# Two blocks of rows (64 and 60 per partition) made into one block of 124 in an elementwise kernel that streams three tensors

## The chip, the cores and the metric

The kernel runs on one core of a Trainium2 chip. The metric is device time in microseconds (us) of one execution. A core has several engines that run side by side, each with its own queue of instructions: here VectorE (DVE) does the arithmetic, TensorE (PE) one small matrix product, and the queues of SyncE (SP) and ScalarE (ACT) issue the DMAs. A DMA moves data between HBM, the large memory, and SBUF, the on-chip memory of 128 partitions; 16 DMA engines carry all DMAs of the core, whichever queue issued them. Engines wait for one another, and for DMAs, by semaphores.

## The reference

```python
B, S, D = 1024, 16, 512
x, y: [B, S, D] bf16;  gamma: [D] bf16

def reference(x, y, gamma):
    return x + gamma * y
```

The three tensors are taken as 16384 rows of 512 numbers. A row is 1 KiB, a tensor 16.8 MB; x and y are read and the output is written, 50.3 MB in all. gamma is the same for each row, so it doesn't matter which partition works on which row, as long as x, y and the output agree.

## The kernel before

Each of the 128 partitions works on 128 rows of y, which all lie in SBUF at once (`y_sb`, 128 KiB a partition, local rows 0 to 127). The result overwrites y there. x has a smaller tile, `x_sb` of 76 rows a partition, whose places are used twice.

*Which rows of the tensors a partition holds* is set by `BLOCKS` (line 7). The tensor is cut into blocks in HBM: the first 4 x 128 rows, then 64 x 128, then 60 x 128. Within a block, partition p has consecutive rows: 4 of the first, 64 of the second, 60 of the third. `rows_of` (line 65) makes the HBM side of a transfer of the local rows a to b: it looks for the block that holds them, views it as "(p n) d -> p n d", and takes the rows from it. Each partition's part of a transfer is one contiguous run in HBM, and the distance from one partition's run to the next, here called the pitch, is the block's rows times 1 KiB:

```python
c = max(c for c in range(len(BLOCKS)) if edges[c] <= a)
assert b <= edges[c + 1]
block = t[P * edges[c] : P * edges[c + 1]].rearrange("(p n) d -> p n d", p=P)
return block[:, a - edges[c] : b - edges[c], :]
```

*The transfers* are two lists in local rows, each the order of one queue. `x` and `y` are loads, `g` the load of gamma, `s` a store; the fourth number of an x load is its place in `x_sb`:

```python
SP  = [('y', 0, 4), ('y', 4, 68), ('x', 4, 68, 4), ('y', 68, 128), ('x', 68, 120, 24), ('x', 120, 128, 0)]
ACT = [('x', 0, 4, 0), ('g',), ('s', 4, 68), ('s', 0, 4), ('s', 68, 128)]
```

`ring` (line 113) issues them. The first two of SP and the first of ACT are moved ahead of the program's opening barriers (`EARLY`, lines 197 to 203); the next ones wait until the load of y rows 0 to 4 has landed (`HOLD`, line 119). The x loads of rows 68 to 120 and 120 to 128 write places of `x_sb` that earlier rows of x had, so each waits on SP for the additions that read those (`frees`, line 102; wait in line 126). The stores wait until the load of x rows 68 to 120 has landed (`RELEASE`, lines 157 to 159 and 123), and each for the additions of its rows. The semaphore waits are made by `_take` (line 32, with the wait itself in line 35).

*The arithmetic* is five pieces of 8, 16, 44, 52 and 8 local rows (`PIECES`), on VectorE alone: `m` multiplies a piece of y by gamma in place (line 180), `a` adds x to it (line 189), in the order `m0 m1 m2 a2 a0 a1 m3 m4 a3 a4`. Before the first multiplication, TensorE spreads gamma over the 128 partitions by a product with a row of ones (line 152), and VectorE copies it to SBUF (line 154). Each piece waits for the loads that bring its rows.

Of the kernel before, what the change touches and what calls it, by code (L numbers as in the profile page):

```python
# [3 lines left out]

BLOCKS = [4, 64, 60]

PIECES = [8, 16, 44, 52, 8]

# [27 lines left out]
def kernel(  # L38
# [22 lines left out]
    dt = xf.dtype  # L61
    edges = [sum(BLOCKS[:c]) for c in range(len(BLOCKS) + 1)]
    assert edges[-1] == rows

    def rows_of(t, a, b):

        c = max(c for c in range(len(BLOCKS)) if edges[c] <= a)
        assert b <= edges[c + 1]
# [165 lines left out]
```

## Time and profile before

| what | value |
|---|---|
| median of 3 runs | 119.66 us (119.55 to 119.72) |
| the profiled execution's span, first to last instruction | 118.2 us |
| first multiplication starts (y rows 4 to 68 landed) | 23.95 us |
| first addition starts (x rows 4 to 68 landed) | 43.45 us |
| last addition ends | 94.4 us |
| stores issued | 77.4, 77.8 and 94.4 us |
| VectorE busy | 70.1 us |

Times in the profile count from the start of the span. The time of a run is longer than the span by what lies around it. "SPq" and "ACTq" are the queues that issue DMAs; q1 and q10 in the table of DMA queues are SP's and ACT's. A DMA is carried out as packets, and a stretch of the DMA table lists the packets that start in it: how many, how many MB, and the time that they took as a share of what 16 engines have in that stretch. The share can be over 100%, since a packet that starts in a stretch may end after it.

### The profile page before, as it was taken

The numbers are of one execution on the slowest core, as the hardware profiler recorded it, in microseconds if no ns is written. First come the engines' busy times: TensorE is split into PE (matmuls) and PEld (weight loads), VectorE is DVE, ScalarE is ACT, GpSimd is POOL, SyncE is SP. The second block draws the span as 40 slices with busy tenths as digits, with TensorE's granted clock in tenths as the row PEclk, the third lists the DMA queues.
The fourth block names the chain that finished last, engine by engine and source line by source line (L and its number), as shares of the span: only waits on it lengthen the run. The fifth ranks groups of instructions, "written<-read, shape, count | busy, mean of one in ns | idle before, by whom it ended". The sixth has DMA issues, their size and how long they took to land. (4 is left out here: it accounts for less than half of the span.)

```text
span 118.2 us, 91 instructions
## 1 busy us (share of the span) xinstructions
PE 0.6 (0%) x1; PEld 0.1 (0%) x1; DVE 70.1 (59%) x12; POOL 0.2 (0%) x4
## 2 busy tenths in 40 slices
PE   0000100000000000000000000000000000000000
PEld 0000000000000000000000000000000000000000
DVE  0000200089999969999999999999999900000000
POOL 0000000000000000000000000000000000000000
DMA  6999889988899879879969696898899889799793
GB/s 248 461 666 399 355 355 399 665 355 355 355 599 466 355 333 624 374 333 499 499 288 576 288 576 288 360 637 355 355 576 488 355 355 510 333 582 416 333 499 166
DMA packets 1442, 50.33 MB, mean 426 GB/s; under 512 B 161, under 2 KB 162, under 8 KB 546
## 3 DMA queue, kind: packets, MB, share of 16 engines
q1 hardware_dynamic: 864, 33.03, 64.8%
q10 hardware_dynamic: 578, 17.30, 33.9%
HBM read 33.56 MB, written 16.78 MB: 426 GB/s over the span
## 5 line engine op out<-in xcount | busy, mean ns | idle before, releaser
L180 DVE TENSOR_TENSOR y_sb<-y_sb,gamma_sb 128x4096 bf16<-128x4096 bf16 (+3 forms) x5 | 34.7, 6981 | 10.9 <-DVEq L35 10.9
L189 DVE TENSOR_TENSOR y_sb<-x_sb,y_sb 128x4096 bf16<-128x4096 bf16 (+3 forms) x5 | 34.7, 6981 | 1.2 <-DVEq L35 1.1
L154 DVE CAST gamma_sb<-gamma_ps 128x512 bf16<-128x512 f32 x1 | 0.7, 692 | 10.2 <-DVEq L35 10.2
L146 DVE MEMSET ones_row<- 1x128 bf16 x1 | 0.2, 165 | 2.0 <-PEq L51 2.0
L152 PE MATMUL gamma_ps<-gamma_row,ones_row 1*128 1x512 bf16 x1 | 0.6, 581 | 11.6 <-PEq L35 11.6
L152 PEld LDWEIGHTS gamma_ps<-gamma_row,ones_row 1*128 1x128 bf16 x1 | 0.1, 101 | 11.6 <-issue 11.6
L218 POOL MEMSET const-bfloat16-1.0<- 128x1 bf16 x1 | 0.1, 101 | 0.0
L218 POOL MEMSET const-uint8-127<- 128x1 uint8 x1 | 0.1, 101 | 0.0
L218 POOL MEMSET const-float32-0.0<- 128x1 f32 x1 | 0.1, 98 | 0.2 <-issue 0.2
L218 POOL MEMSET const-float32-1.0<- 128x1 f32 x1 | 0.1, 98 | 0.0
## 6 DMA issues: line engine op xcount, KB each, us to landing
y_sb<-in_y_dram SPq DMA_DIRECT2D x1, 7680.0 KB, 57.3
out_dram<-y_sb ACTq DMA_DIRECT2D x1, 7680.0 KB, 23.8
x_sb<-in_x_dram SPq DMA_DIRECT2D x1, 6656.0 KB, 21.7
x_sb<-in_x_dram SPq DMA_DIRECT2D x1, 1024.0 KB, 22.0
y_sb<-in_y_dram SPq DMA_DIRECT2D x1, 512.0 KB, 3.4
x_sb<-in_x_dram ACTq DMA_DIRECT2D x1, 512.0 KB, 4.2
out_dram<-y_sb ACTq DMA_DIRECT2D x1, 512.0 KB, 22.3
y_sb<-in_y_dram SPq DMA_DIRECT2D x1, 23.4
```

The costliest lines, as they stand in the source:

```text
L146: nc.vector.memset(ones_row, 1.0).then_inc(s_ones, 1)
L152: nc.tensor.matmul(gamma_ps, ones_row, gamma_row, start=True, stop=True).then_inc(s_ps, 1)
L154: nc.vector.tensor_copy(out=gamma_sb, in_=gamma_ps).then_inc(s_dve, 1)
L180: nc.vector.tensor_tensor(out=yt, in0=yt, in1=g, op=MULT).then_inc(s_dve, 1)
L189: nc.vector.tensor_tensor(out=yt, in0=xt, in1=yt, op=ADD).then_inc(s_add, 1)
L218: nc = _bacc.Bacc("TRN2", target_bir_lowering=False, num_devices=1)
```

## The change

```diff
-BLOCKS = [4, 64, 60]
+BLOCKS = [4, 124]
```

Nothing else is edited. Behind the first block, partition p now has 124 consecutive rows of the tensors: its local rows 4 to 128. The lists of transfers, in local rows, stay as they are, so a transfer of rows 4 to 68 takes the first 64 of a partition's 124 rows, and one of rows 68 to 128 the last 60. The pitch is 124 KiB for all transfers but those of rows 0 to 4, where it was 64 KiB (rows 4 to 68) or 60 KiB (rows 68 to 128). Before, a transfer of rows 4 to 68 covered one contiguous region of HBM from the first to the last byte; now there are 60 KiB between the runs of neighbouring partitions.

## The prediction

> **What bounds the kernel now.** I read the page's slices first, then its table of queues, then the DMA issues with their time to landing, and last the DMA table again for stretches that hold packets of one transfer alone. From the page:
>
> ```profile
> span 118.2 us, 91 instructions
> PE 0.6 (0%) x1; PEld 0.1 (0%) x1; DVE 70.1 (59%) x12; POOL 0.2 (0%) x4
> DMA  6999889988899879879969696898899889799793
> DMA packets 1442, 50.33 MB, mean 426 GB/s; under 512 B 161, under 2 KB 162, under 8 KB 546
> q1 hardware_dynamic: 864, 33.03, 64.8%
> q10 hardware_dynamic: 578, 17.30, 33.9%
> ```
>
> The two queues' packets fill 64.8 + 33.9 = 98.7% of what 16 DMA engines have in the span. Only the first slice (nothing has arrived) and the last one are much below full. A 7 or a 6 in the middle is not a hole: the profile puts a long packet down in the slice where it starts, and the neighbouring slice shows it (GB/s swings between 288 and 666 likewise). VectorE works 59% of the time. So the kernel lasts as long as the sum of its packets. VectorE would matter only if one of its waits held back an issue until the queues ran dry, and that is read from the issues:
>
> ```profile
> y_sb<-in_y_dram SPq DMA_DIRECT2D x1, 7680.0 KB, 57.3
> out_dram<-y_sb ACTq DMA_DIRECT2D x1, 7680.0 KB, 23.8
> x_sb<-in_x_dram SPq DMA_DIRECT2D x1, 6656.0 KB, 21.7
> out_dram<-y_sb ACTq DMA_DIRECT2D x1, 512.0 KB, 22.3
> 55.37 2.53 SPq L132 DMA_DIRECT2D x_sb<-in_x_dram  x2
> 77.41 17.36 ACTq L138 DMA_DIRECT2D out_dram<-y_sb  x3
> ```
>
> The last two lines are from the timeline (start, duration). The load of x rows 68 to 120 waits for VectorE and is issued at 55.4, while y rows 68 to 128, issued at 4.1, land at 4.1 + 57.3 = 61.4: 6 us of cover. The last store is issued at 77.41 + 17.36 - 0.3 = 94.4, while the store of rows 0 to 4, issued at 77.8, lands at 77.8 + 22.3 = 100.1: 5.7 us of cover. The chain of waits names two additions of VectorE and "issue"; it stops at the last addition, which ends 24 us before the span does, so it doesn't tell what bounds.
>
> The price of one packet, from the DMA table cut to stretches (us), in this order: 3.6 to 23 (y rows 4 to 68), 24 to 42 (x rows 4 to 68), 44 to 60 (y rows 68 to 128), 62 to 74 (x rows 68 to 120), 81 to 98 (store of rows 4 to 68), 101 to 115 (store of rows 68 to 128):
>
> ```profile
> q1 hardware_dynamic: 128, 8.39, 100.4%
> ...
> q1 hardware_dynamic: 112, 7.34, 94.1%
> ...
> q1 hardware_dynamic: 112, 6.88, 99.4%
> ...
> q1 hardware_dynamic: 96, 5.11, 98.3%
> ...
> q10 hardware_dynamic: 112, 7.34, 99.6%
> ...
> q10 hardware_dynamic: 96, 5.90, 97.2%
> ```
>
> Each line has packets, MB and the share of 16 engines. 19.4 us x 16 x 1.004 / 128 = 2.435 us a packet; by the same working 2.420, 2.272, 1.966, 2.419 and 2.268 us. MB over packets gives 65.5, 61.4 and 53.2 KB: one packet is the whole run of one partition (64, 60 or 52 rows of 1 KiB), 128 packets a transfer, 8 on each of 16 engines. In bytes per ns and engine these are 26.9, 27.1, 27.0, 27.1, 27.1 and 27.1. So one rate holds for loads and stores and for a pitch (distance in HBM from one partition's run to the next) of 64 KiB and of 60 KiB.
>
> **The change part by part.** It *removes and adds* no instruction: on every engine the built program has the same instructions in the same order, shapes and waits. No step moves past another on SP, ACT or any queue, and the tile in SBUF keeps its places, since rows 0 to 128 of a partition stay where they were; each partition merely holds other rows of the tensors. What changes is the HBM side of seven transfers: the pitch goes from 64 KiB (three of them) and 60 KiB (four) to 124 KiB, and the start moves for the 60-row part. The run of one partition stays contiguous, 64, 60, 52 or 8 rows. The three transfers of rows 0 to 4 and gamma are untouched.
>
> Seven transfers of 8 packets per engine, priced by the rows above (for the 8-row load 1.966 x 8 / 52 = 0.30): 8 x (2.435 + 2.420 + 2.272 + 1.966 + 0.30 + 2.419 + 2.268) = 8 x 14.08 = 112.6 us of the span's 118.2. That is all the change can touch; the other 5.6 us are the start, the 4-row transfers and the last landing.
>
> *Number of packets: no change, 0 us.* A packet was one partition's run already in the blocks of 64, where neighbouring partitions touch in HBM and longer packets would have been possible; the new layout gives the same runs.
>
> *Price of a packet at a pitch of 124 KiB: not shown by this trace.* Bound below: the cheapest row is 27.1 bytes per ns. The stores show it, and so do most loads; if all reached it, y rows 4 to 68 would give back 8 x (2.435 - 2.419) = 0.13 us, x rows 4 to 68 0.01, y rows 68 to 128 8 x (2.272 - 2.268) = 0.03: some 0.17 in all. Bound above: the dearest. A stretch from 3.6 to 6 us, the first round of packets after the queues fill, has
>
> ```profile
> q1 hardware_dynamic: 16, 1.05, 103.4%
> ```
>
> so 2.4 x 16 x 1.034 / 16 = 2.482 us a packet, 2.6% over 2.419; on all 112.6 us that is +2.9. Between these I take 0. One of the two pitches shown is a power of two (64 KiB) and one is not (60 KiB), as 124 KiB is not; they differ by nothing in stores and by 0.2% or less in the later loads. The one dear transfer is the first big one, dearest in its first round, while x rows 4 to 68 with the same pitch pay 2.420: that goes by when it runs, not by where it lies, so the pitch doesn't remove it.
>
> The row of the first transfer also bears on a rule: the Trainium skill (DMA: Bandwidth & Descriptors, Latency and other measured facts) says that copies whose partitions lie a large power of two apart lose rate, 207 GB/s at 512 KiB against 214 at a padded pitch, and advises padding by a few KiB or laying tiles out contiguously. The change goes against the second half (the blocks of 64 were contiguous as a whole) and with the first (124 KiB is no power of two). With the page's 3% as an estimate for a bad pitch the sum would be +3.5 us or so; the rows at 64 and 60 KiB, equal within 0.2% in steady state, say about 0, and no row has 124 KiB.
>
> *Waits.* Unchanged in number. If packets grow, the waits of VectorE move with them: its first multiplication starts at 23.95 on the landing of y rows 4 to 68 and would start later by 8 times the growth; the covers of 6 and 5.7 us shift along with the transfers, so they hold.
>
> Sum: 118.2 + 0 in the span. The median of the runs is 119.66, 1.4 us above the span, for what lies around it; that stays. Forecast 119.66, with its own range 119.45 to 119.85.
>
> **Rivals.** (A) *The new pitch makes streams collide in HBM* (slower). In the blocks as they are, the 16 engines read a region of 8 MB as a whole; now they read stretches with gaps in 16 MB, and 16 engines stand at multiples of another distance. For it: the first round's 2.6% shows that packets can be stretched when 16 start together. Against: after that round no row is over 0.4%, for either pitch. There is no slack, so every per cent of packet price is 1.1 us; over 0.24 us it takes 0.21%. At the first transfer's whole-length row (26.9 against 27.1, 2.435 over 2.419 = 0.66%) on all 112.6 us: +0.74, 120.4; at its row after the first round (6 to 23 us: 112 packets at 100.0%, 2.429, 0.4%): +0.46, 120.1; on the first round's price: 122.6.
>
> (B) *Runs are cut at boundaries of the HBM address*, so that the change does add packets. Runs at a pitch of 60 KiB already cross multiples of 64 KiB, whole, which speaks against it. A stretch of small packets prices it: from 98.3 to 99.25 us, 103 packets (97 of 4 KB, the rest a few bytes) fill 101.8%, so 0.15 to 0.16 us each, against 4096 / 27.1 = 0.151: about 8 ns of their own. 56 more per engine: +0.45, 120.1.
>
> (C) *The first transfer's loss is a matter of the layout and goes away* (faster): -0.17, 119.49, which would still count as no change; to pass 0.24 every packet must also run faster than the best row. The stores, equal at both pitches, speak against that: their price looks like the engines' own.
> The Trainium skill's ceiling (DMA: Bandwidth & Descriptors, Where 436 GB/s comes from) is 435.2 GB/s for the 16 engines together; the best rows have 27.1 x 16 = 433.4, so by the page even a perfect layout would win an estimated 0.4%, 0.5 us.
>
> **How the numbers follow.** A measurement of this kernel can tell about 0.2% (0.24 us) from no change; the three runs lie within 0.17. Forecast 0.57, A 0.29, B 0.04, C 0.10. Slower is A and B, 0.33. Of C I give 0.07 to faster, for packet prices under any row shown, and 0.03 to the same: 0.60. The time is the forecast's. The range goes from 119.40, under C's price with the runs' scatter, to 120.40, which takes in A's two steady prices and B; left out are A towards its first-round price, 0.13, and the far end of C, 0.04.
>
> **What would show it.** Right: again 1442 packets; the same stretches within 0.2% of 2.419 and 2.268 us a packet; y rows 4 to 68 landing near 23.8, x rows 4 to 68 near 43.2, y rows 68 to 128 near 61.4, the last store near 118.2. A shows as packets that grow in some or all of the seven transfers, with landings that fall behind step by step and queues still full. B shows in the packet count alone. C shows as the first landing coming some 0.1 us early. The forecast is wrong if the price of a packet depends on the pitch where 60 and 64 KiB were too alike to show it, or if reads and stores differ in that.

## The result and the profile after

| what | before | after |
|---|---|---|
| median | 119.69 us (119.55 to 119.72, 5 runs) | 120.05 us (119.87 to 120.24, 5 runs) |
| profiled execution: run | not told | 119.87 us |
| its span | 118.2 us | 118.5 us |

The ratio is 1.0032, with a 95% interval of 1.0022 to 1.0043: the change costs 0.36 us. The profile of after is of its fastest run.

The page of after, the lines that answer to those of before:

```profile
span 118.5 us, 91 instructions
PE 0.6 (0%) x1; PEld 0.1 (0%) x1; DVE 70.1 (59%) x12; POOL 0.2 (0%) x4
DMA  6999888988899879979969697898899889798792
DMA packets 1442, 50.33 MB, mean 425 GB/s; under 512 B 161, under 2 KB 162, under 8 KB 546
q1 hardware_dynamic: 864, 33.03, 64.9%
q10 hardware_dynamic: 578, 17.30, 33.8%
y_sb<-in_y_dram SPq DMA_DIRECT2D x1, 7680.0 KB, 57.3
out_dram<-y_sb ACTq DMA_DIRECT2D x1, 7680.0 KB, 23.9
x_sb<-in_x_dram SPq DMA_DIRECT2D x1, 6656.0 KB, 21.8
```

The number of packets and their bytes are the same, and so is VectorE's busy time. The queues are as full as they were (64.9 + 33.8 = 98.7%) of a longer span. The DMAs shown land 0 to 0.1 us later after their issue.

The six stretches of the DMA table of after, in the order of the prediction (from 3.6, 24, 44, 62, 81 and 101 us; packets, MB, share of 16 engines):

```profile
q1 hardware_dynamic: 128, 8.39, 100.2%
...
q1 hardware_dynamic: 112, 7.34, 94.2%
...
q1 hardware_dynamic: 112, 6.88, 99.5%
...
q1 hardware_dynamic: 96, 5.11, 98.5%
...
q10 hardware_dynamic: 112, 7.34, 99.6%
...
q10 hardware_dynamic: 96, 5.90, 97.2%
```

The two stores stand to the digit where they stood. The loads have +0.1 or +0.2 points in three stretches and -0.2 in the first. On the mean over 16 engines, then, this profile hardly shows the loss. It shows in when things land. From the timeline, the multiplications, the first of which waits for y rows 4 to 68 (start of the first, busy time), in before and then in after:

```profile
23.95 18.43 DVE L180 TENSOR_TENSOR y_sb<-y_sb,gamma_sb 128x4096 bf16<-128x4096 bf16 x3 [10.94 <-DVEq L35]
```
```profile
24.14 18.43 DVE L180 TENSOR_TENSOR y_sb<-y_sb,gamma_sb 128x4096 bf16<-128x4096 bf16 x3 [10.98 <-DVEq L35]
```

From the chain of waits, the piece of VectorE that ends with the landing of x rows 120 to 128 (start, duration), again in before and then in after:

```profile
78.17 1.41 DVE y_sb L189
```
```profile
78.34 1.52 DVE y_sb L189
```

The multiplication starts 0.19 us later. From there to the last load's landing it was 78.17 + 1.41 - 23.95 = 55.63 us and is 78.34 + 1.52 - 24.14 = 55.72. So 0.19 us are lost up to the first big load, 0.09 in the loads after it, and the few hundredths that are left of the span's 0.3 in the stores' last landings. (The 0.19 turns out below to be within what equal kernels differ by.) Each wait for a load is for 16 signals; of the 16 for y rows 4 to 68 in before, the first came at 23.43 us and the last at 23.81. So a transfer has landed when the slowest part is there, and that time, not the mean, makes these waits.

### The profile page after: what moved, and what is told of

It reads as the page before. It is cut to its first block, busy times and chain, and to the rows that moved or that the text cites. A ratio compares the mean times of both kernels' runs of the same rounds, so it can differ in the third digit from the quotient of the medians.

```text
span 118.5 us, 91 instructions
## 1 busy us (share of the span) xinstructions
PE 0.6 (0%) x1; PEld 0.1 (0%) x1; DVE 70.1 (59%) x12; POOL 0.2 (0%) x4
## 2 busy tenths in 40 slices
DMA packets 1442, 50.33 MB, mean 425 GB/s; under 512 B 161, under 2 KB 162, under 8 KB 546
## 3 DMA queue, kind: packets, MB, share of 16 engines
q1 hardware_dynamic: 864, 33.03, 64.9%
q10 hardware_dynamic: 578, 17.30, 33.8%
```

## The experiments

Each kernel was run 6 to 12 times beside the kernel before on the same chip (23 to 35 runs of that). The kernels of one section below ran on one chip; the five sections had five chips, called 6, 2, 3, 13 and 12 here. Which chip the first measurement had isn't known, so "three chips" in an expectation means three measurements. Differences are of medians. The ratios, with their 95% intervals, follow all runs and so needn't agree with the medians: for the four later loads on chip 6 the medians are 0.01 us apart to the fast side, the means 0.08 to the slow one. To move single transfers, `rows_of` was given the kind of the transfer, and a list tells which ones take the other layout:

```diff
+OTHER = [4, 124]
+MOVED = [('y', 4), ('x', 4), ('y', 68), ('x', 68), ('x', 120)]
...
-    def rows_of(t, a, b):
+    def rows_of(t, a, b, kind):
...
-        c = max(c for c in range(len(BLOCKS)) if edges[c] <= a)
-        assert b <= edges[c + 1]
-        block = t[P * edges[c] : P * edges[c + 1]].rearrange("(p n) d -> p n d", p=P)
-        return block[:, a - edges[c] : b - edges[c], :]
+        cut = OTHER if (kind, a) in MOVED else BLOCKS
+        edge = [sum(cut[:c]) for c in range(len(cut) + 1)]
+        c = max(c for c in range(len(cut)) if edge[c] <= a)
+        assert b <= edge[c + 1]
+        block = t[P * edge[c] : P * edge[c + 1]].rearrange("(p n) d -> p n d", p=P)
+        return block[:, a - edge[c] : b - edge[c], :]
```

Each call of `rows_of` passes `kind`. Below, only `MOVED` (and `OTHER`, where it is another) is shown. Where only some transfers are moved, the output has other rows than the reference's; the transfers and the arithmetic are as many as before. Packets over the price that most packets of their size have are called long; that price is called the floor.

### Loads against stores, the first big load against the later ones (chip 6)

```diff
+MOVED = [('y', 4), ('x', 4), ('y', 68), ('x', 68), ('x', 120)]
```


> The five loads behind row 4 take the 124 KiB pitch, the two stores keep 64 and 60 KiB (so x and y rows that meet in a partition are stored to other rows than the reference has). Theory L (the loads pay for the pitch, the stores do not): all of the loss, +0.3 to +0.4 us over the kernel before. Theory S (the stores pay, in landings rather than in packets): 0, within 0.1. Theory B (a share each): about half, +0.2.

```diff
+MOVED = [('s', 4), ('s', 68)]
```


> The two stores alone take the 124 KiB pitch, all loads are as before (the output has other rows in places). Theory L: 0, within 0.1 us of the kernel before. Theory S: +0.3 to +0.4. Theory B: about +0.2.

```diff
+MOVED = [('y', 4)]
```


> Only the load of y rows 4 to 68, the first big transfer, takes the 124 KiB pitch (y meets other rows of x). Theory F (the loss is made in the first microseconds, when the 16 engines leave the 4-row loads and start this transfer together): most of it, +0.25 to +0.4 us, and the landing of y rows 4 to 68 is later by 0.2. Theory E (each load pays a little): a quarter of it, under +0.15.

```diff
+MOVED = [('x', 4), ('y', 68), ('x', 68), ('x', 120)]
```


> The four loads after the load of y rows 4 to 68 take the 124 KiB pitch, that one and the stores do not (x and y rows don't match). Theory F: nearly nothing, under +0.1 us. Theory E: most of the loss, +0.2 to +0.3, with x rows 4 to 68, y rows 68 to 128 and x rows 68 to 120 each landing a little later against the one before it.

| moved | difference | ratio | highest run |
|---|---|---|---|
| all five loads | +0.06 us | 1.0010 (1.0002 to 1.0018) | 120.33 |
| both stores | -0.08 | 0.9994 (0.9986 to 1.0003) | 119.89 |
| y rows 4 to 68 | -0.03 | 0.9999 (0.9991 to 1.0008) | 119.92 |
| the four later loads | -0.01 | 1.0006 (0.9997 to 1.0015) | 120.27 |

No run of the kernel before was over 119.94 here. No theory met all its numbers: the loads cost something, but a third of what the first measurement had by the ratio and a sixth by the medians, and more in a few long runs than in the median. The changed kernel itself did not run on this chip, so how much there was to share out here isn't known. What falls is theory S. The stores cost nothing, in time and in packets; the stretches 81 to 98 and 101 to 115 us of the profile with the stores moved:

```profile
q10 hardware_dynamic: 112, 7.34, 99.6%
...
q10 hardware_dynamic: 96, 5.90, 97.2%
```

These are the shares of before at 64 and 60 KiB.

### The changed kernel again, an equal kernel, and two other cuts (chip 2)

The first two are the changed kernel and the kernel before, unedited. The others:

```diff
-BLOCKS = [4, 64, 60]
+BLOCKS = [128]
```
and
```diff
-BLOCKS = [4, 64, 60]
+BLOCKS = [68, 60]
```

> The changed kernel itself, timed beside the kernel before on one chip in many runs. Theory P (the pitch of 124 KiB makes loads dearer, wherever it runs): +0.36 us as in the first measurement, at the least +0.25. Theory N (the first measurement's +0.36 is for a part the scatter of the first loads, 5 runs against 5): +0.1 us, as the loads alone gave, and single runs that reach up to 120.3.

> The kernel before under a label of its own: a second profile of it, and a measure of how far equal kernels differ. Theory P: the first loads of 4 rows cost what they did in its first profile (0.09 us over their floor). Theory N: they cost what they did in the changed kernel's profile, 0.2 to 0.35 us, without any change of layout. The time is the same as the kernel before's, within 0.1.

> One block of 128 rows: the pitch is 128 KiB, a power of two, for every load and store, those of the 4 rows too, whose runs of 4 KiB then lie 128 KiB apart. Theory C (streams collide by pitch, more at a power of two): +0.5 us or more, in packets of all loads. Theory N: 0 to +0.2, for a pitch does not matter once the first loads are through.

> Blocks of 68 and 60: only the first two blocks are joined, so rows 0 to 4 and 4 to 68 have a pitch of 68 KiB and the rest is as before. Theory H (gaps between the runs of the first loads cost, at the start alone): +0.1 to +0.3 us, all of it before the landing of x rows 0 to 4. Theory N: within 0.1.

| kernel | difference | ratio | runs |
|---|---|---|---|
| the changed one | +0.38 us | 1.0029 (1.0013 to 1.0045) | 119.72 to 120.82 |
| the kernel before | +0.10 | 1.0005 (0.9996 to 1.0014) | 119.64 to 119.99 |
| one block of 128 | +0.26 | 1.0022 (1.0013 to 1.0032) | 119.90 to 120.13 |
| blocks of 68 and 60 | +0.25 | 1.0018 (1.0009 to 1.0027) | 119.83 to 120.05 |

The loss of the changed kernel is there again, so theory N in its simple form (a matter of 5 runs against 5) falls. But it is half right about the profiles: in the second profile of the kernel *before*, the first multiplication starts at

```profile
24.27 2.29 DVE L180 TENSOR_TENSOR y_sb<-y_sb,gamma_sb 128x4096 bf16<-128x4096 bf16 x1 [10.95 <-DVEq L35]
```

That is later than in the changed kernel's (24.14). The 0.19 us of the first pair of profiles at this place is within what equal kernels differ by.

The second profile of the changed kernel has a part of the loss where the mean shows it, in x rows 4 to 68 (24 to 42 us, 112 packets; 94.1% in both profiles of before):

```profile
q1 hardware_dynamic: 112, 7.34, 94.8%
```

18 x 16 x 0.948 / 112 = 2.438 us a packet against 2.420. And the chain of waits of that profile has

```profile
78.43 1.63 DVE y_sb L189
```

so the last load lands at 80.06, half a microsecond later than in before's first profile (79.58). Before's second profile, however, has

```profile
78.47 1.42 DVE y_sb L189
```

and lands it at 79.89, because its first big load was late. From the first multiplication (24.15 us in the changed kernel's profile) to this landing it is 55.91 us in the changed kernel and 55.62 in the kernel before: 0.29 us are lost there.

One block of 128 stays far under theory C's +0.5 and is a little over theory N's +0.2.

The blocks of 68 and 60 tell something else, near what theory H said: when the 4-row loads' runs have gaps, the loss is made at once. The table of this kernel from 1 to 2.85 us, and from 3.6 to 23:

```profile
q1 hardware_dynamic: 110, 0.45, 87.1%
...
q1 hardware_dynamic: 128, 8.39, 99.7%
```

The same 1.85 us in before's first and second profile:

```profile
q1 hardware_dynamic: 138, 0.52, 73.8%
```
```profile
q1 hardware_dynamic: 127, 0.52, 75.1%
```

That is 1.85 x 16 x 0.738 / 138 = 0.158 us a packet and 0.175 by the same working, here 0.234. Eighteen of the profiles in this study have 4-row loads as before; they have 0.158 to 0.207. The load of x rows 0 to 4 has landed by 4.34 to 4.57 us in those and at 4.87 here. y rows 4 to 68 then take 19.4 x 16 x 0.997 / 128 = 2.418 us a packet, the stores' price, with gaps of 4 KiB between their runs. Their first round (3.6 to 6 us), which the prediction met at 2.482, is at the floor too. First this kernel, then the one measured below in which the same load has the same pitch of 68 KiB but the 4-row loads are as before:

```profile
q1 hardware_dynamic: 16, 1.05, 100.8%
```
```profile
q1 hardware_dynamic: 16, 1.05, 103.7%
```

By the working of the prediction it takes 2.441 to 2.513 us a packet in all eighteen profiles with the 4-row loads as before. So the dear first round isn't a property of that transfer's layout: it goes by the loads ahead of it. That also gives back a part of the 0.3 us and more by which the 4-row loads are late.

### On one chip: the whole, the loads, the later loads, and 128 KiB (chip 3)

The changed kernel, two of the lists that ran on chip 6 (all five loads, the four later ones), and all five loads with

```diff
+OTHER = [128]
+MOVED = [('y', 4), ('x', 4), ('y', 68), ('x', 68), ('x', 120)]
```

> The changed kernel once more, on the same chip as its parts below. Theory L (the loads pay, and chips or placements differ in how much): +0.1 to +0.4 us, the same as the loads alone on this chip, within 0.1. Theory X (loads and stores pay only together): +0.36 here, and 0.1 for the loads alone.

> The five loads at 124 KiB, the stores as before. Theory L: as the changed kernel in this call, within 0.1 us. Theory X: 0.1 over the kernel before, 0.25 under the changed kernel.

> The four loads after y rows 4 to 68 at 124 KiB, that one and the stores as before. Theory L, with a loss made in the later loads: as the loads all together, within 0.1 us, and single runs over 120.1. If the loss is made in the first big load: 0 within 0.1, and no run over 120.1.

> The five loads behind row 4 take a pitch of 128 KiB (each partition's rows 4 to 128 of 128 consecutive ones); the 4-row transfers and the stores stay as before, so the outputs are of other rows. Theory G (any pitch that leaves gaps between runs makes later loads dearer): +0.1 to +0.4 us, as the 124 KiB loads. Theory O (it depends on the offset between the 16 engines' streams, which at 128 KiB is a power of two as it was at 64): within 0.1 of the kernel before.

| kernel | difference | ratio | runs |
|---|---|---|---|
| the changed one | +0.41 us | 1.0041 (1.0025 to 1.0056) | 119.95 to 120.61 |
| five loads at 124 KiB | +0.33 | 1.0031 (1.0015 to 1.0046) | 119.71 to 120.78 |
| four later loads at 124 KiB | +0.11 | 1.0007 (0.9999 to 1.0016) | 119.62 to 120.09 |
| five loads at 128 KiB | +0.15 | 1.0016 (1.0007 to 1.0025) | 119.58 to 120.16 |

Theory L holds: by the medians the loads alone make the changed kernel's loss, within 0.1 us, on the chip where both ran (the two intervals overlap over most of their width, so a small share of the stores isn't excluded by the times). Theory X falls. The median of the later four alone doesn't make it here. One execution of theirs did, though, the profiled one (120.09 us): x rows 120 to 128 landed in it 0.41 us later after y rows 4 to 68 than in before, and some 0.2 of that is in these 8 rows alone. 128 KiB costs too, so theory O falls, but it needn't be theory G: see 68 KiB below.

The trace shows how such a loss looks. The 16 packets of x rows 68 to 120 that start between 68 and 69.5 us, in before and then in the changed kernel's third profile:

```profile
q1 hardware_dynamic: 16, 0.85, 131.1%
```
```profile
q1 hardware_dynamic: 16, 0.85, 134.0%
```

2.9% of 1.5 x 16 us is 0.70 us more for the sixteen. By the trace's records of single packets it lies in four of them: 0.29, 0.25, 0.08 and 0.07 us over the floor of 1.966 us; the others have next to nothing. A few packets are hit, and hard. With the loads at 128 KiB it is a whole round of y rows 68 to 128, each packet by 0.04 to 0.28 us (44 to 46 us, 16 packets; before has 113.4% in this stretch):

```profile
q1 hardware_dynamic: 16, 0.98, 120.6%
```

### Shares of the two loads of rows 4 to 68, and a small gap (chip 13)

```diff
+MOVED = [('y', 4)]
```


> Only y rows 4 to 68 at 124 KiB. Theory V (each load that leaves the old pitch pays its share, by the offset of the 16 streams): a quarter of the changed kernel's loss, about 0.1 us. Theory W (the whole start with the first big load pays): two thirds or more, 0.25. Theory J (what pays is the spread between engines that builds up over several loads): 0, with runs no wider than the kernel before's.

```diff
+MOVED = [('y', 4), ('x', 4)]
```


> y and x rows 4 to 68 at 124 KiB, the 60-row block's loads and the stores as before (x and y agree, but the first block's results go to other rows). Theory V: half of the loss, about 0.2. Theory W: the same as y rows 4 to 68 alone. Theory J: little, under 0.15, the rest coming with the loads of rows 68 to 128.

```diff
+OTHER = [68, 60]
+MOVED = [('y', 4), ('x', 4)]
```


> The loads of y and x rows 4 to 68 at a pitch of 68 KiB, with gaps of 4 KiB between runs, the rest as before (results of the first block go to other rows). Theory gap (any gap costs): +0.1 to +0.2 us. Theory distance (the offset of the 16 streams decides, and 68 KiB is good, as the blocks of 68 showed: no packet of these loads over its floor): 0 to -0.1 us, with y rows 4 to 68 within 0.03 us of its floor.

and the changed kernel beside them:

> The changed kernel on the chip of the three parts below: +0.3 to +0.45 us over the kernel before by what three chips gave; +0.1 if this chip is mild.

| kernel | difference | ratio | runs |
|---|---|---|---|
| the changed one | +0.07 us | 1.0009 (0.9999 to 1.0018) | 119.74 to 120.19 |
| y rows 4 to 68 | +0.03 | 1.0003 (0.9995 to 1.0012) | 119.73 to 120.01 |
| y and x rows 4 to 68 | 0.00 | 1.0000 (0.9991 to 1.0008) | 119.71 to 119.90 |
| those two at 68 KiB | +0.02 | 1.0004 (0.9995 to 1.0012) | 119.73 to 120.13 |

The whole change was mild here, so the shares are told for a mild case alone: rows 4 to 68 cost nothing that shows, at 124 KiB or at 68 (the intervals end at 0.15 us or less). Theory W isn't met on this chip, but with a whole of 0.07 us its two thirds wouldn't show either; it stays open for a chip on which the loss is large. A gap of 4 KiB costs nothing that shows. Theory distance isn't met: the pitch of 68 KiB gains nothing, and leaves the first round dear (103.7% above), once the 4-row loads are as before.

### The loads of rows 68 to 128 alone (chip 12)

```diff
+MOVED = [('y', 68), ('x', 68), ('x', 120)]
```

> Only the three loads of rows 68 to 128 take 124 KiB; all loads of rows 0 to 68 and all stores are as before (x and y agree, the results of the last block go to other rows). Theory T (these loads make the loss, in single packets of one engine): as the changed kernel in this call, within 0.1 us, with packets over 0.06 us too long in x rows 68 to 120. Theory J (the spread of the engines from the earlier loads at 124 KiB is needed too): under a half of the changed kernel's loss, where that is 0.3 or more.

> The changed kernel on the chip of the run below: either +0.1 us (as on two chips) or +0.36 to +0.41 (as on three).

The changed kernel: +0.19 us, ratio 1.0022 (1.0010 to 1.0034), runs of 119.77 to 120.56. These three loads alone: +0.11 us, 1.0010 (1.0001 to 1.0019), 119.73 to 120.21. By its limit of 0.1 us theory T is met, but the profile shows none of the long packets in x rows 68 to 120 that T asked for, and 0.11 of 0.19 us is hardly more than the half under which theory J would be met, had the loss been the 0.3 us or more that J asks for. This one decides nothing but that these loads cost something, and that barely (the interval starts at 1.0001).

### All profiles together

Three parts of the span, from the times at which the DMAs' semaphores were complete: until y rows 4 to 68 have landed, from there until x rows 120 to 128 have, and from there to the end. The last column counts packets of 52 to 64 KiB that start after 24 us and took more than 0.06 us over their floor (2.418 us at 64 KiB and 2.267 at 60, the stores' price; 1.966 at 52 KiB, the price in before).

```
later loads at         kernel                        run us   until  between  to end  long
64 (68) and 60 KiB     before                        -        23.81  55.72    38.66   0
                       before, again                 119.85   24.14  55.70    38.65   1
                       stores moved                  119.75   23.99  55.71    38.69   1
                       y 4-68 moved                  119.79   24.06  55.73    38.64   0
                       y 4-68 moved, again           119.76   24.04  55.71    38.66   0
                       blocks of 68 and 60           119.96   24.23  55.72    38.65   0
                       y and x 4-68 at 68 KiB        119.84   24.11  55.71    38.67   0
124 KiB, all or part   y and x 4-68 moved            119.84   24.11  55.72    38.66   4
                       rows 68-128 moved             119.73   23.95  55.76    38.67   1
                       four later loads              119.68   23.92  55.76    38.64   0
                       four later loads, again       120.09   23.90  56.13    38.70   3
                       five loads                    119.83   24.10  55.72    38.65   1
                       five loads, again             119.95   24.07  55.83    38.69   5
                       changed kernel, 1st           119.87   24.00  55.81    38.70   5
                       changed kernel, 2nd           120.06   24.01  56.00    38.70   24
                       changed kernel, 3rd           119.95   24.00  55.92    38.68   7
                       changed kernel, 4th           119.83   24.00  55.78    38.69   3
                       changed kernel, 5th           119.79   24.07  55.71    38.65   0
128 KiB                five loads at 128 KiB         120.11   24.04  56.03    38.68   49
                       one block of 128              120.13   24.44  55.70    38.63   13
```

The middle part is the sharpest reading in this study. Where the later loads keep their pitch, or have one of 68 KiB, it is 55.70 to 55.73 us in seven profiles. With the later loads at 124 KiB it is 55.71 to 56.13, on the mean of the ten such profiles (all in that group but the first) 55.84, so 0.13 us more, and where it is much more there are long packets, in the last column and, for the 56.13, in the last 8 rows too. "Until" scatters by 0.3 us in kernels that start alike, and "to end", which holds the stores, by 0.07.

The middle part accounts for what the profiled executions lost. The five of the changed kernel took 119.90 us on the mean; the four of kernels that start as before and keep the later loads' pitch (before again, stores moved, y 4-68 moved twice) took 119.79. That is 0.11 us, against 0.13 in the middle part.

The long runs of the changed kernel were not caught: of 47 runs of the changed kernel in five measurements 13 are over 120.12 us, of 126 runs of the kernel before beside them none, and the slowest profiled execution of the changed kernel took 120.06.

## Why the prediction was wrong

**What bounds: right.** The queues stayed full, VectorE's waits moved with the landings, and its covers weren't used up. Since nothing is hidden, a loss of 0.1 us in the loads shows in the time, as the comparison by parts has just shown.

**The number of packets: right.** 1442 again. That ended rival B; C ended with the first comparison. (That longer packets "would have been possible" is shown by no run: none has one over 64 KiB.)

**The price of a packet at 124 KiB: the step that failed.** The prediction put this term at 0, between -0.17 and +2.9 us: "One of the two pitches shown is a power of two (64 KiB) and one is not (60 KiB), as 124 KiB is not; they differ by nothing in stores and by 0.2% or less in the later loads." From two pitches that agreed it took a third to agree. The runs showed +0.36, +0.38, +0.41, +0.07 and +0.19 us for the changed kernel in five measurements, and +0.33 for its five loads alone where the whole gave +0.41. The time of 120.05 lies inside the range given, but the range reached that far for rival A, which had a chance of 0.29. Two of the reasons given were too weak. Stores, which agree at every pitch tried, were counted as witnesses for loads. And 60 and 64 KiB have more in common than a good price: at both, the runs of neighbouring partitions touch, or leave 8 rows between them in the load of x rows 68 to 120. The trace of before has one load with wide gaps, x rows 120 to 128 (runs of 8 KiB, 52 KiB between them), but it lasts some 2.5 us and was priced by scaling another row. The prediction's last line named this way to be wrong, 60 and 64 KiB "too alike", and its sum gave it no time.

**The mean over 16 engines was the wrong view for it.** The prediction's sign of being right was 2.419 and 2.268 us a packet "within 0.2%". By it nothing could be told: the first transfer had 2.435 in before and has 2.430 in after (19.4 x 16 x 1.002 / 128), and no stretch of after is more than 0.2 points from before, at a loss. The share of 16 engines dilutes what one engine loses by 16, while the landing waits for the slowest. Nor did the landings tell as they were named, by their time from the start: in two executions of the kernel before, y rows 4 to 68 landed at 23.81 and at 24.14 us, so that rival C's "some 0.1 us early" couldn't have been seen either. What told was the time from one landing to another.

**Rival A was the way it went,** and its steady prices (+0.46 and +0.74) were of the right size though too high. But its mechanism, streams that collide in HBM, is only argued: what is shown is long packets in loads, single ones, some, or a whole round, mostly in places that change from one execution to the next. One place recurs: between 68.4 and 69.3 us, in x rows 68 to 120, all five profiles of the changed kernel but the last have one to four of them, both of the five loads at 124 KiB have some, and so has the kernel with only the stores moved (one, of 0.09 us). So not every long packet comes from the pitch, and why that place is hit isn't known.

**When against where.** The dear first round of y rows 4 to 68 was said to go by when it runs. For this the runs speak: at 124 KiB that load alone costs nothing that shows (0.9999 and 1.0003), and at one and the same pitch of 68 KiB its first round is dear behind the 4-row loads of before (103.7%) and at the floor behind slower ones (100.8%).

**The rule on pitches** (Trainium skill, DMA: Bandwidth & Descriptors, Latency and other measured facts) was set aside because 60 and 64 KiB agreed. Its advice to lay tiles out contiguously points the way the loads went, though 68 KiB, with gaps, cost nothing that shows. Its figure at 512 KiB, 207 GB/s against 214, is for a pitch that no run here has; the estimate of +3.5 us that the prediction made of it is far over what 124 KiB cost, 0.1 to 0.4% of the time.

**What stays open.** Which loads make the full loss: on the chip with +0.41 us the five loads gave +0.33 and the later four +0.11, and the first one wasn't tried there alone; on the other chips the parts are too small to add up. Why the measurements differ, from 1.0009 to 1.0041: by chip, by where the tensors lay in HBM (which no run varied on its own), or by chance of few long runs. And what the changed kernel's long runs, over 120.1 us, hold.

## What to carry to other kernels

When the DMA engines are full from end to end, a layout that changes only addresses can still cost: price it with a row that has the same layout, and where there is none, don't let agreeing rows of other layouts, or stores, stand for it. Read the times between landings beside shares, because the slowest of 16 engines ends a transfer. For effects under half a per cent take several profiles of the same kernel first, to know which parts of the span repeat to 0.03 us and which scatter by 0.3.

## What the runs showed of the hardware

- The very first loads are worth their contiguity: the 4-row loads of SP's queue, in 4 KiB runs, cost 0.158 to 0.207 us a packet from 1 to 2.85 us in the eighteen profiles where these runs touch, 0.234 where they lie 68 KiB apart and 0.230 where they lie 128 KiB apart. x rows 0 to 4 land by 4.34 to 4.57 us in the first and at 4.87 and 5.04 in the other two, and these two kernels are 0.25 and 0.26 us slower as a whole (1.0018 and 1.0022; an equal kernel beside them was 0.10 slower, 1.0005).
- Stores never varied: 99.6% and 97.2% in the same stretches in all twenty profiles, at pitches of 60 to 128 KiB.
- Loads at 128 KiB had a round at 120.6% of its stretch against 113.4% in one kernel, and in the kernel with one block of 128 the same loads took 55.70 us from landing to landing, as in before, with 13 long packets among them. With one profile of each, whether the slower start of the second one spared it or chance did isn't shown.
